# First mixture in six sub-runs of 400 and 384 tokens instead of eight of 300

## The chip, the cores and the metric

The kernel runs on one core of one Trainium2 chip. The core's engines are TensorE (PE, with PEld for its weight loads), VectorE (DVE), ScalarE (ACT), GpSimd (POOL) and SyncE (SP, which issues most transfers). The metric is the device time of one launch in microseconds (us). Three timed runs of the kernel before gave 945.01, 948.21 and 948.75 us, median 948.21.

## The reference

Attention with a memory term (4 batches, 8 heads, 576 positions, head size 64), then a mixture of 8 experts over the 2304 tokens, each token through one expert only, then a dense gated layer over all tokens:

```
local   = softmax(causal(q k^T / 8)) v
mem_out = (phi(q) M_prev) / (phi(q) z_prev + 1e-6)      # phi(x) = elu(x) + 1
x       = sigmoid(beta) * mem_out + (1 - sigmoid(beta)) * local      # -> 2304 x 512
logits  = x w_gate + modality_bias[modality_id]
e       = argmax(logits);   p = softmax(logits)[e]
out1    = p * (relu(x w1[e]) w2[e])                     # 512 -> 1024 -> 512
out     = (silu(out1 w_gate2) * (out1 w_val)) w_out     # 512 -> 1536 -> 512
```

With the inputs that are timed, all tokens fall to two of the eight experts, 1173 to the one and 1131 to the other.

## The kernel before

Three stages follow one another on the core. Matrix products are made of fp32 values split in two parts, high and low (three matmuls for one product: high by high, high by low, low by high), so a "block" of work on TensorE comes in threes.

Stage 1 is the attention: 16 pairs of heads, four for each batch. When a batch's pairs are done, `route` computes its gate logits, chooses the expert of each token and writes row numbers, sorted by expert, to a table in device memory (`idsE`). The order of all work is set when the program is built: class `Sched` is a planner which holds every piece with an engine, a planned duration, the pieces it needs, the buffers it takes from pools, and a priority. It goes through planned time and writes the pieces out; each engine executes its own in that order. A table `PRM` (line 32) holds one offset of priority for each kind of piece in stage 1.

Stage 2 is the first mixture. Each chosen expert's rows are computed in `NS=4` sub-runs of `W=300` rows. After three of the four batches are routed, the expert with most rows is chosen, and the first `NE=2` of its sub-runs take rows of those three batches; so they are prepared inside stage 1, and computed while the routing of the last batch goes on. A sub-run is in two functions. `rows` (L642) loads its row numbers (L646), transposes them on TensorE (L647), gathers the rows by three indirect transfers that POOL issues (L652), transposes these on TensorE (L654), and splits them: ACT writes the high part (L657), DVE the low one (L658). `sub` (L661) walks eight blocks of the hidden layer: 12 matmuls (L682 to L684) give `h` for 128 hidden units, ACT writes `hh` (L686), DVE `hl` (L687), then 12 matmuls (L670 to L672) add the block's part to the four outputs `y`. TensorE does h0, h1, y0, h2, y1 and so on: 192 matmuls, 300 columns each. At the end the outputs leave PSUM (L693) and go to memory (L696), and the row numbers after them (L697). The function `rest` would run on, in a loop on the chip, for rows that do not fit the eight sub-runs.

The weights of the experts come in as fp32 and are split by ACT and by POOL or DVE (`split`, L620). The dense layer's weights come in a 64-bit form; twelve of these tiles are decoded in stage 2, in two halves each (`split64`, L623 to L640).

Stage 3 is the dense layer, six tiles of 384 tokens, with outputs scattered to their rows. The change leaves it alone but for the places of a few buffers.

The planner's start rule, which decides among pieces, is unchanged; the functions that the change touches follow.

Of the kernel before, what the change touches and what calls it, by code (L numbers as in the profile page):

```python
# [176 lines left out]
class Net:  # L177
    W=300; NS=4; NE=2; TN=384
    TP=16000.; US=PRM['US']
    def __init__(s,tc,A):  # L180
        s.tc=tc; s.nc=tc.nc; s.A=A
        s.B,s.H,s.S,s.D=A['q'].shape; s.HP=s.H//2; s.NP=s.B*s.HP
        s.T=s.B*s.S; s.E=A['moe_w_gate'].shape[1]; s.dm=A['moe_w_gate'].shape[0]; s.F1=A['moe_w1'].shape[2]; s.F2=A['moe2_w_gate'].shape[1]
        s.CAP=s.W*s.NS; s.R=s.T+s.CAP
# [5 lines left out]
    def consts(s,pc,pa):  # L190
# [8 lines left out]
        s.wg=T(pc,"wg",[128,4,48]); s.mi=T(pa,"mi",[128,B,5,2],I32); s.mb2=T(pa,"mb2",[128,2,E]); s.mf=T(pa,"mf",[128,2,B*5])  # L199
        s.bias=T(pc,"bias",[128,B*5,E]); s.bias2=T(pa,"bias2",[128,B*5,E]); s.cum=T(pc,"cum",[128,B*5+1,E],BF)  # L200
# [282 lines left out]
    def route(s,b):  # L483
# [105 lines left out]
    def slots(s):  # L589
# [3 lines left out]
        s.pick(7,8,3,float(s.CAP))  # L593
# [50 lines left out]
    def rows(s,row,deps,prio,ph,ps,name='',nb=None):  # L644
        nc=s.nc; sc=s.sc; n=s.W//3; it,ii,xh,xl=sc.tok('it'),sc.tok('ii'),sc.tok('xh'),sc.tok('xl'); tp0=sc.tok(ps)
        d=sc.dma(lambda: s.after('ids',nc.sync.dma_start(out=it.tile,in_=s.idsE[bass.ds(row(),s.W),:].rearrange("(a c) o -> a (c o)",a=3))),deps=deps[0],acq=[it],prio=prio,name='id'+name,ph=ph,late=4500. if ph==1 else 3500.)  # L646
        a=sc.add('PE',10,lambda: nc.tensor.transpose(tp0.tile[0:n,0:3],it.tile,s.ident[0:3,0:3]),deps=[d],acq=[tp0],use=[it],prio=prio+.1,name='it'+name,ph=ph)  # L647
# [13 lines left out]
    def sub(s,rw,w1,w2,col,prio,ph,wr,name=''):  # L661

        nc=s.nc; sc=s.sc; W=s.W; it,xh,xl,xd=rw; ys=[sc.tok(f'y{d}') for d in range(4)]; st=24600./8; NF=s.F1//128; ylast=[]
        prev=None; yT=[]
# [11 lines left out]
        for fb in range(NF):  # L676
            wh,wl,wd=w1[fb//2]; hp=sc.tok('h'); hh,hl=sc.tok('hh'),sc.tok('hl')
            def f(wh=wh,wl=wl,hp=hp,fb=fb):
                fs=slice(128*(fb%2),128*(fb%2)+128); o=hp.tile[:,0:W]
                for k in range(4):  # L680
                    H=wh.tile.rearrange("p (k f) -> p k f",k=4)[:,k,fs]; Lo=wl.tile.rearrange("p (k f) -> p k f",k=4)[:,k,fs]
                    nc.tensor.matmul(o,H,xh.tile[:,k],start=(k==0),stop=False)  # L682
                    nc.tensor.matmul(o,H,xl.tile[:,k],start=False,stop=False)  # L683
                    nc.tensor.matmul(o,Lo,xh.tile[:,k],start=False,stop=(k==3))  # L684
# [1 line left out]
            b=sc.add('ACT',ac(W),lambda hp=hp,hh=hh: nc.scalar.activation(out=hh.tile,in_=hp.tile[:,0:W],func=AF.Relu),deps=[a],acq=[hh],use=[hp],prio=prio+fb*st,name=f'hh{name},{fb}',ph=ph)  # L686
            c=sc.add('DVE',dv(W),lambda hp=hp,hh=hh,hl=hl: nc.vector.scalar_tensor_tensor(out=hl.tile,in0=hp.tile[:,0:W],scalar=0.0,in1=hh.tile.bitcast(F32),op0=ALU.max,op1=ALU.subtract),deps=[b],acq=[hl],use=[hp,hh],prio=prio+fb*st,name=f'hl{name},{fb}',ph=ph)  # L687
# [251 lines left out]
```

## Time and profile before

| what | us |
|---|---|
| median of three timed runs | 948.21 |
| the profiled execution | 954.26 |
| its span in the trace | 952.5 |
| TensorE busy | 921.6 (97%) |
| VectorE busy | 491.4 (52%) |
| ScalarE busy | 388.7 (41%) |
| GpSimd busy | 177.3 (19%) |
| stage 1, start to 247.7 | 247.7 |
| stage 2, 247.7 to 488.0 | 240.3 |
| stage 3, 488.0 to the end | 464.5 |

The profiled execution is one of its own, 6.05 us above the median of the timed ones, so its terms are counted against its own time. TensorE's matmuls are pipelined: one lasts longer than the distance to the next start, and the sum of the engine's work is read from the distance of starts.

### The profile page before, as it was taken

The page shows a single profiled execution, that of the slowest core. Times are in us where ns is not written, and L with a number is a line of the kernel's source. Part 1 is how long each engine was busy: PE and PEld are TensorE (multiplying, and loading weights), DVE is VectorE, ACT ScalarE, POOL GpSimd, SP SyncE. Part 2 cuts the span into 40 slices and gives each one's busy share as a digit, 9 for nine tenths or more (in the row PEclk, how much of TensorE's full clock was granted, in tenths as well). Part 3 has the DMA queues.
Part 4 walks back from the last instruction along what each step waited for, and adds up shares of the span by engine and source line. Part 5 has one row for each costly group of instructions (what it writes and reads, how often), then busy time and mean ns, then how long its engine had stood idle before and what let it go on. Part 6 is the DMA issues. An engine that isn't in the chain of part 4 may idle for free. (4 is left out here: it accounts for less than half of the span.)

```text
span 952.5 us, 16582 instructions
## 1 busy us (share of the span) xinstructions
PE 921.6 (97%) x6389; PEld 841.0 (88%) x6389; DVE 491.4 (52%) x1382; ACT 388.7 (41%) x902; POOL 177.3 (19%) x199
## 2 busy tenths in 40 slices
PE   8999999999899899999989999999999999999996
PEld 6787787877799899999989999999999999999995
DVE  7988888887542728832558862232223223222221
ACT  6888888788424334411424431121122112111111
POOL 3112111125427324311212220001001001001001
PEclk9999999999999999999999999999999999999999
DMA  6632437124266425441233320001001000000000
GB/s 137 135 75 53 109 85 116 28 40 150 93 83 216 144 87 172 141 144 53 84 114 123 111 65 25 1 20 47 1 0 67 1 1 34 1 1 34 1 1 34
DMA packets 93424, 67.27 MB, mean 71 GB/s; under 512 B 67514, under 2 KB 78924, under 8 KB 93341
## 3 DMA queue, kind: packets, MB, share of 16 engines
q1 hardware_dynamic: 88797, 56.37, 23.0%
q0 software_dynamic: 4544, 9.79, 3.2%
q8 instruction: 52, 0.85, 0.4%
q14 instruction: 31, 0.25, 0.1%
HBM read 51.65 MB, written 14.49 MB: 69 GB/s over the span
## 5 line engine op out<-in xcount | busy, mean ns | idle before, releaser
L796 DVE SCALAR_TENSOR_TENSOR X<-X,gv 128x384 f32<-128x384 f32 x72 | 39.9, 554 | 186.4 <-ACT X L795 186.4
L787 PE MATMUL gv<-xx,wB 128*128 128x384 f32 x384 | 130.7, 340 | 2.0 <-PEq L822 2.0
L789 PE MATMUL gv<-xx,wB 128*128 128x384 f32 x384 | 130.7, 340 | 0.0
L788 PE MATMUL gv<-xx,wB 128*128 128x384 f32 x384 | 130.7, 340 | 0.0
L795 ACT ACTIVATE X<-gv 128x384 f32<-128x384 f32 x72 | 35.4, 491 | 190.0 <-PE gv L789 176.9
L422 ACT ACTIVATE PF<-SS,sm 128x256 f32<-128x256 f32 (+1 forms) x144 | 87.3, 609 | 9.5 <-DVE sm L410 7.0
L606 POOL DMA_INDIRECT out_dram<-X,ii x18 | 17.5, 973 | 368.8 <-ACT X L814 366.2
L787 PEld LDWEIGHTS gv<-xx,wB 128*128 128x128 f32 x384 | 72.5, 189 | 4.3 <-issue 2.2
L788 PEld LDWEIGHTS gv<-xx,wB 128*128 128x128 f32 x384 | 72.5, 189 | 2.0
L789 PEld LDWEIGHTS gv<-xx,wB 128*128 128x128 f32 x384 | 72.6, 189 | 0.0
L687 DVE SCALAR_TENSOR_TENSOR hl<-h,hh 128x300 fp32r<-128x300 f32 x64 | 30.0, 468 | 81.9 <-ACT hh L686 81.6
L797 DVE TENSOR_TENSOR X<-X,gv 128x384 f32<-128x384 f32 x72 | 39.9, 554 | 61.1 <-PE gv L789 60.9
L410 DVE CUSTOM_DVE_ANT_0 SS<-ps,mk 128x256 f32<-128x256 f32 (+2 forms) x128 | 64.8, 518 | 7.9 <-PE ps L402 5.7
L686 ACT ACTIVATE hh<-h 128x300 fp32r<-128x300 f32 x64 | 26.7, 418 | 91.3 <-PE h L684 85.5
L432 PE MATMUL tp<-ident,PF 128*128 128x128 f32 x384 | 61.7, 281 | 1.7 <-ACT pt L438 1.3
L438 ACT ACTIVATE pt<-tp 128x512 f32<-128x512 f32 (+2 forms) x112 | 55.0, 506 | 16.1 <-PE tp L432 13.9
L683 PE MATMUL h<-xx,wB 128*128 128x300 f32 x192 | 57.6, 300 | 1.5 <-DVE xx L658 1.5
L682 PE MATMUL h<-xx,wB 128*128 128x300 f32 x192 | 57.9, 302 | 0.0
L684 PE MATMUL h<-xx,wB 128*128 128x300 f32 x192 | 57.6, 300 | 0.0
L807 PE MATMUL po<-wB,al 128*128 128x512 f32 x144 | 56.7, 394 | 0.0
L432 PEld LDWEIGHTS tp<-ident,PF 128*128 128x128 f32 x384 | 43.5, 141 | 8.8 <-ACT pt L438 3.6
L670 PE MATMUL y<-hh,wB 128*128 128x300 f32 x160 | 49.1, 307 | 1.0 <-DVE X L693 1.0
(287 smaller groups left out, 2337.8 us busy)
## 6 DMA issues: line engine op xcount, KB each, us to landing
raw<-in_moe_w_dram SPq DMA_DIRECT2D x16, 512.0 KB
raw<-in_moe_w_gate_dram SPq DMA_DIRECT2D x12, 512.0 KB
raw<-in_moe_w_val_dram SPq DMA_DIRECT2D x12, 512.0 KB
raw<-in_moe_w_out_dram SPq DMA_DIRECT2D x12, 512.0 KB
yT<-X SPq DMA_DIRECT2D x8, 600.0 KB
X<-yT SPq DMA_DIRECT2D x6, 768.0 KB
kn<-in_k_dram SPq DMA_DIRECT2D x32, 128.0 KB
qn<-in_q_dram SPq DMA_DIRECT2D x32, 128.0 KB
```

Source lines behind the costliest of these rows:

```text
L410: def f(Sp=Sp,SS=SS,i=i,N=N,c=c,so=so): nc.vector.tensor_tensor_reduce(out=SS.tile[:,0:N],in0=Sp.tile[:,so:so+N],in1=s.mk[:,512-128*i:512- ...
L422: def f(SS=SS,PF=PF,N=N,c=c): nc.scalar.activation(out=PF.tile[:,0:N],in_=SS.tile[:,0:N],func=AF.Exp,scale=-1.0,bias=sm.tile[:,c:c+1],accu ...
L432: for j in range(m+1): nc.tensor.transpose(tp.tile[:,128*j:128*j+128],PF.tile[:,128*j:128*j+128],s.ident)
L438: else: cps.append(add('ACT',ac(W),lambda pc=pc,tv=tv: nc.scalar.activation(out=pc(),in_=tv(),func=AF.Copy),deps=[Tt],prio=pu+2*US,name=f' ...
L670: nc.tensor.matmul(o,H,hh.tile,start=(fb==0),stop=False)
L682: nc.tensor.matmul(o,H,xh.tile[:,k],start=(k==0),stop=False)
L683: nc.tensor.matmul(o,H,xl.tile[:,k],start=False,stop=False)
L684: nc.tensor.matmul(o,Lo,xh.tile[:,k],start=False,stop=(k==3))
L787: nc.tensor.matmul(o,H,yh.tile[:,k],start=(k==0),stop=False)
L788: nc.tensor.matmul(o,H,yl.tile[:,k],start=False,stop=False)
L789: nc.tensor.matmul(o,Lo,yh.tile[:,k],start=False,stop=(k==3))
L807: nc.tensor.matmul(o,lv()[:,c],H,start=False,stop=(f==NF-1))
```

## The change

The first mixture's sub-runs become 400 rows wide and three for each expert. The second expert's take 384 rows (`W1`), so all six hold 3 x 400 and 3 x 384 rows where eight held 300 each. The rows of a sub-run come in `G` groups of at most 128: four of 100, or three of 128. The write of the row numbers (`iw`) now waits for the load of the same numbers and the write before it, and its priority is six tenths of a sub-run ahead of the sub-run. The pools are dealt out anew for the wider tiles: two `hh` and two `hl` instead of three, two `it` instead of three, the buffers of the last stage in other places of the tiles X0 and X1. The gate's matmul has 32 columns instead of 48. All offsets in `PRM` are new, so the whole order of stage 1 is.

```diff
...
-    'AV,5':6, 'AV,7':-5.67, 'AV,8':-4.47, 'S,0':4.42, 'S,2':5.94, 'S,3':4.15, 'S,8':3.99, 'T,0':-5.64, 'T,1':-5.59, 'T,2':-3.75, 'T,3':-5.07,
+    'AV,5':-5.84, 'AV,7':-5.21, 'AV,8':-1.56, 'S,0':5.11, 'S,2':5.25, 'S,3':5.41, 'S,8':4.95, 'T,0':-6, 'T,1':-3.05, 'T,2':-1.59, 'T,3':-3.46,
...
-    W=300; NS=4; NE=2; TN=384
+    W=400; NS=3; NE=2; TN=384
...
-        s.CAP=s.W*s.NS; s.R=s.T+s.CAP
+        s.CAP=s.W*s.NS; s.R=s.T+s.CAP; s.W1=s.T//2//s.NS; s.CAP1=s.W1*s.NS
...
-        s.wg=T(pc,"wg",[128,4,48]); s.mi=T(pa,"mi",[128,B,5,2],I32); s.mb2=T(pa,"mb2",[128,2,E]); s.mf=T(pa,"mf",[128,2,B*5])
+        s.wg=T(pc,"wg",[128,4,32]); s.mi=T(pa,"mi",[128,B,5,2],I32); s.mb2=T(pa,"mb2",[128,2,E]); s.mf=T(pa,"mf",[128,2,B*5])
...
-                    for c in range(0,m,64): nc.tensor.matmul(lg.tile[c:c+64,0:48],xt.tile[:,k,c:c+64],s.wg[:,k],start=(k==0),stop=(k==3))
+                    for c in range(0,m,64): nc.tensor.matmul(lg.tile[c:c+64,0:32],xt.tile[:,k,c:c+64],s.wg[:,k],start=(k==0),stop=(k==3))
...
-        s.pick(7,8,3,float(s.CAP))
+        s.pick(7,8,3,float(s.CAP1))
...
-        nc=s.nc; sc=s.sc; n=s.W//3; it,ii,xh,xl=sc.tok('it'),sc.tok('ii'),sc.tok('xh'),sc.tok('xl'); tp0=sc.tok(ps)
+        nc=s.nc; sc=s.sc; W=W or s.W; G=-(-W//128); n=W//G; it,ii,xh,xl=sc.tok('it'),sc.tok('ii'),sc.tok('xh'),sc.tok('xl'); tp0=sc.tok(ps)
...
-        for j in range(3):
+        for j in range(G):
...
+        iw=sc.dma(lambda: nc.sync.dma_start(out=s.ids[bass.ds(col(),W),:].rearrange("(a c) o -> a (c o)",a=G),in_=it.tile[0:G,0:n]),deps=[idd]+wr[-1:],use=[it],prio=prio-.6*s.ST,name='iw'+name,ph=ph)
...
-        wr.append(sc.dma(lambda: nc.sync.dma_start(out=s.ids[bass.ds(col(),W),:].rearrange("(a c) o -> a (c o)",a=3),in_=it.tile),deps=wr[-1:]+wr[-2:-1],use=[it],prio=prio+9.3*st,name='iw'+name,ph=ph))
+        wr.append(iw)
...
-        for q in range(8):
-            if q>=2: s.rw[q]=s.rows(R[q],([rg]+sd,xw),st*(q-.7),2,'xp',f'{q}')
-            s.sub(s.rw[q],s.w1[q//4],s.w2[q//4],C[q],st*q,2,s.wr,f'{q}')
+        for q in range(2*NS):
+            if q>=NE: s.rw[q]=s.rows(R[q],([rg]+sd,xw),S2*(q-.7),2,'xp',f'{q}',W=W if q<NS else W1)
+            s.sub(s.rw[q],s.w1[q//NS],s.w2[q//NS],C[q],S2*q,2,s.wr,f'{q}')
...
-        s.tiles(pc,'it',3,[3,W//3]); s.tiles(pc,'ii',2,[128,3],I32)
-        xx=[pc.tile([128,4,TN],F32R,name=f"xx{i}") for i in range(4)]
+        s.tiles(pc,'it',2,[4,128]); s.tiles(pc,'ii',2,[128,4],I32)
+        xx=[pc.tile([128,4*W],F32R,name=f"xx{i}") for i in range(4)]
...
-            s.tiles(p2,'hh',3,[128,W],F32R); s.tiles(p2,'hl',3,[128,W],F32R)
+            s.tiles(p2,'hh',2,[128,W],F32R); s.tiles(p2,'hl',2,[128,W],F32R)
...
```
In the order on POOL at the end of stage 1 before, the rows of the second prepared sub-run (row numbers ii1) are gathered in three pieces, with splits of weights (L620) behind them; X1 is the last batch's output, xr the gathered rows:

```order
L472 TENSOR_TENSOR X1_84<-t10_133,t20_134 128x4x128
L652 DMA xr0_98<-xg_59,ii0_78 100x512
L652 DMA xr1_99<-xg_59,ii0_78 100x512
L652 DMA xr2_100<-xg_59,ii0_78 100x512
L652 DMA xr3_101<-xg_59,ii1_79 100x512
L620 TENSOR_TENSOR w3_69<-raw0_73,w0_66 128x1024
L472 TENSOR_TENSOR X1_84<-t10_133,t20_134 128x4x128
L652 DMA xr0_98<-xg_59,ii1_79 100x512
L652 DMA xr1_99<-xg_59,ii1_79 100x512
L620 TENSOR_TENSOR w5_71<-raw1_74,w1_67 128x1024
L620 TENSOR_TENSOR HL_72<-raw2_104,w2_68 128x1024
L472 TENSOR_TENSOR X1_84<-t10_133,t20_134 128x4x128
```

The same place on POOL after, with line numbers of the changed file (gathers L654, splits L621):

```order
L473 TENSOR_TENSOR X1_83<-t10_132,t20_133 128x4x128
L654 DMA xr0_97<-xg_59,ii0_77 100x512
L654 DMA xr1_98<-xg_59,ii0_77 100x512
L654 DMA xr2_99<-xg_59,ii0_77 100x512
L654 DMA xr3_100<-xg_59,ii0_77 100x512
L473 TENSOR_TENSOR X1_83<-t10_132,t20_133 128x4x128
L621 TENSOR_TENSOR w1_67<-raw0_73,w0_66 128x1024
L621 TENSOR_TENSOR w3_69<-raw1_74,w2_68 128x1024
L654 DMA xr0_97<-xg_59,ii1_78 100x512
L654 DMA xr1_98<-xg_59,ii1_78 100x512
L654 DMA xr2_99<-xg_59,ii1_78 100x512
L654 DMA xr3_100<-xg_59,ii1_78 100x512
```

All four gathers of the second sub-run now stand behind two splits, where one of three stood ahead of one split and the other two ahead of the next two.

On TensorE, the end of stage 1 before; L654 transposes gathered rows, L432 to L445 are the attention's last pieces, L682 is the first matmul of stage 2:

```order
L654 MATMUL ps2_142<-ident_148,xr3_101 128x100 x4
L441 MATMUL mm0_147<-ident_148,PF0_122 128x128
L432 MATMUL tp0_143<-ident_148,PF0_122 128x128 x4
L467 MATMUL tp1_144<-ident_148,oT0_132 128x128 x4
L445 MATMUL mm0_147<-vn10_110,pt41_131 64x64 x10
L654 MATMUL ps1_141<-ident_148,xr0_98 128x100 x4
L654 MATMUL ps0_140<-ident_148,xr1_99 128x100 x4
L491 MATMUL xp0_3377<-ident_148,X1_84 128x128 x4
L682 MATMUL h0_3375<-xx0_80,w0_66 128x300
```

And after:

```order
L656 MATMUL ps0_139<-ident_147,xr3_100 128x100 x4
L442 MATMUL mm0_146<-ident_147,PF0_121 128x128
L433 MATMUL tp0_142<-ident_147,PF0_121 128x128 x4
L468 MATMUL tp1_143<-ident_147,oT0_131 128x128 x4
L446 MATMUL mm0_146<-vn10_109,pt41_130 64x64 x10
L656 MATMUL ps1_140<-ident_147,xr0_97 128x100 x4
L656 MATMUL ps2_141<-ident_147,xr1_98 128x100 x4
L656 MATMUL ps0_139<-ident_147,xr2_99 128x100 x4
L656 MATMUL ps1_140<-ident_147,xr3_100 128x100 x4
L492 MATMUL xp0_3390<-ident_147,X1_83 128x128 x4
L685 MATMUL h0_3388<-xx0_79,w0_66 128x400
```

Between the attention's last piece and the first matmul of stage 2 stand four groups of transposes instead of two.

## Rows read from the trace of the kernel before

**Rows 1.** Stretches: us, busy of PE, PEld, DVE, ACT, POOL (instructions), clock, DMA, GB/s.
```profile
0.00:225.00 225.00, 217.69 (x2160) 174.03 (x2161) 189.61 (x807) 186.66 (x511) 46.93 (x80) 1.00 0.43 92
225.00:247.70 22.70, 17.19 (x151) 14.36 (x149) 16.33 (x41) 13.88 (x32) 14.58 (x10) 0.85 0.37 114
247.70:488.00 240.30, 230.47 (x1706) 225.65 (x1707) 122.20 (x255) 86.92 (x170) 80.69 (x63) 0.99 0.42 117
```

**Rows 2.** Timeline of PE: start, us, operation, count [idle before <-releaser].
```profile
270.35 0.30 PE L670 MATMUL y<-hh,wB 128*128 128x300 f32 x1
...
275.33 0.30 PE L682 MATMUL h<-xx,wB 128*128 128x300 f32 x1
...
519.20 0.34 PE L787 MATMUL gv<-xx,wB 128*128 128x384 f32 x1
...
523.44 0.39 PE L805 MATMUL po<-wB,ah 128*128 128x512 f32 x1
```

**Rows 3.** Timeline of PE: transposes of gathered rows and of full tiles.
```profile
182.28 1.04 PE L491 MATMUL ps<-ident,X 128*128 128x128 f32 x8
...
384.15 0.85 PE L654 MATMUL xp<-ident,xr 100*128 100x100 f32 x8
```

**Rows 4.** Timeline of PE: two waits for the third sub-run's rows.
```profile
288.39 0.21 PE L647 MATMUL xp<-ident,it 3*100 3x3 f32 x1 [1.32 <-DMA it<-idsE]
...
310.30 0.41 PE L682 MATMUL h<-xx,w 128*128 128x300 f32 x1 [0.46 <-ACT xx L657]
```

**Rows 5.** Timeline of DVE, tail of stage 1.
```profile
233.11 0.16 DVE L382 TENSOR_TENSOR dn<-dn,gate 128x6 f32<-128x6 f32 x1
...
236.34 4.77 DVE L382 TENSOR_TENSOR dn<-dn,gate 128x4 f32<-128x4 f32 x1
```

**Rows 6.** Timeline of POOL, tail of stage 1.
```profile
234.06 1.01 POOL L652 DMA_INDIRECT xr<-xg,ii  x1 [2.05 <-PE ps L654]
235.38 1.01 POOL L652 DMA_INDIRECT xr<-xg,ii  x1 [0.31 <-PE ps L654]
236.42 2.37 POOL L620 TENSOR_TENSOR w<-raw,w 128x1024 fp32r<-128x1024 f32 x1
238.73 2.35 POOL L620 TENSOR_TENSOR HL<-raw,w 128x1024 fp32r<-128x1024 f32 x1
```

**Rows 7.** Timeline of PE, tail of stage 1.
```profile
234.84 0.64 PE L377 MATMUL mm<-mb,qp 128*128 128x130 f32 x4
...
238.72 0.56 PE L654 MATMUL ps<-ident,xr 100*128 100x100 f32 x4
242.07 0.30 PE L441 MATMUL mm<-ident,PF 128*128 128x128 f32 x1 [2.79 <-DVE t L390]
...
245.16 1.18 PE L654 MATMUL ps<-ident,xr 100*128 100x100 f32 x8
```

**Rows 8.** Two stretches at a lower granted clock, columns as in rows 1.
```profile
242.36:245.77 3.41, 3.41 (x33) 2.96 (x31) 2.48 (x9) 1.54 (x2) 1.00 (x1) 0.50 0.38 121
317.46:320.87 3.41, 3.41 (x16) 3.41 (x15) 3.02 (x4) 0.58 (x2) 1.45 (x1) 0.50 0.69 216
```

**Rows 9.** Timeline of DVE, of POOL and of PE around 314.
```profile
312.24 3.14 DVE L634 TENSOR_SCALAR X<-X 128x512 int32<-128x512 int32 x1
...
312.69 2.41 POOL L620 TENSOR_TENSOR wB<-raw,wB 128x1024 fp32r<-128x1024 f32 x1
...
316.54 0.40 PE L672 MATMUL y<-hl,w 128*128 128x300 f32 x1 [1.92 <-DVE hl L687]
```

**Rows 10.** Page's groups: busy, mean ns | idle before and its releaser.
```profile
L687 DVE SCALAR_TENSOR_TENSOR hl<-h,hh 128x300 fp32r<-128x300 f32 x64 | 30.0, 468 | 81.9 <-ACT hh L686 81.6
...
L686 ACT ACTIVATE hh<-h 128x300 fp32r<-128x300 f32 x64 | 26.7, 418 | 91.3 <-PE h L684 85.5
```

**Rows 11.** Line L682 with its shapes: count, ns least/median/most, first and last start.
```profile
L682 PE MATMUL h<-xx,wB x192: 295/299/408, 265.3 to 480.4; 128*128 128x300 f32 x192
...
L682 PE MATMUL h<-xx,w x64: 295/301/453, 247.7 to 352.0; 128*128 128x300 f32 x64
```

More of the change, by code (lines that the diff above doesn't have):

```diff
@@ L32 @@
 PRM={'US': 1807, 'slack': 69, 'ps': (3, 2, 1, 1, 1), 'dcopy': (0,), 'off':{
[10 rows of a table removed]
[5 rows of a table added]
+    'gate':4.72, 'gx':5.91, 'ic':1.15, 'id':6, 'it':4.18, 'kHi':-0.09, 'kLo':3.5, 'kT':0.25, 'ldk':-0.67, 'ldm':-6, 'ldq':0.47, 'ldv':4.2, 'ldz':-1.77,
[4 rows of a table added]
 NW=24; NC=4
@@ L642, in w2src, with rows @@
     def w2src(s,er,j): w=s.A['moe_w2'].rearrange("e f d -> (e f) d"); return lambda: w[bass.ds(s.er[er]*s.F1+256*j,256),:].rearrange("(k p) d -> p k d",p=128)
-    def rows(s,row,deps,prio,ph,ps,name='',nb=None):
-        nc=s.nc; sc=s.sc; n=s.W//3; it,ii,xh,xl=sc.tok('it'),sc.tok('ii'),sc.tok('xh'),sc.tok('xl'); tp0=sc.tok(ps)
-        d=sc.dma(lambda: s.after('ids',nc.sync.dma_start(out=it.tile,in_=s.idsE[bass.ds(row(),s.W),:].rearrange("(a c) o -> a (c o)",a=3))),deps=deps[0],acq=[it],prio=prio,name='id'+name,ph=ph,late=4500. if ph==1 else 3500.)
-        a=sc.add('PE',10,lambda: nc.tensor.transpose(tp0.tile[0:n,0:3],it.tile,s.ident[0:3,0:3]),deps=[d],acq=[tp0],use=[it],prio=prio+.1,name='it'+name,ph=ph)
-        a=sc.add('DVE',75,lambda: nc.vector.tensor_copy(ii.tile[0:n],tp0.tile[0:n,0:3]),deps=[a],acq=[ii],use=[tp0],prio=prio+.2,name='ic'+name,ph=ph)
+    def rows(s,row,deps,prio,ph,ps,name='',nb=None,W=None):
+        nc=s.nc; sc=s.sc; W=W or s.W; G=-(-W//128); n=W//G; it,ii,xh,xl=sc.tok('it'),sc.tok('ii'),sc.tok('xh'),sc.tok('xl'); tp0=sc.tok(ps)
+        d=sc.dma(lambda: s.after('ids',nc.sync.dma_start(out=it.tile[0:G,0:n],in_=s.idsE[bass.ds(row(),W),:].rearrange("(a c) o -> a (c o)",a=G))),deps=deps[0],acq=[it],prio=prio,name='id'+name,ph=ph,late=4500. if ph==1 else 3500.)
+        a=sc.add('PE',10,lambda: nc.tensor.transpose(tp0.tile[0:n,0:G],it.tile[0:G,0:n],s.ident[0:G,0:G]),deps=[d],acq=[tp0],use=[it],prio=prio+.1,name='it'+name,ph=ph)
+        a=sc.add('DVE',75,lambda: nc.vector.tensor_copy(ii.tile[0:n,0:G],tp0.tile[0:n,0:G]),deps=[a],acq=[ii],use=[tp0],prio=prio+.2,name='ic'+name,ph=ph)
@@ L649, in rows @@
         dd=[]
-        for j in range(3):
+        wv=lambda t: t.tile[:,0:4*W].rearrange("p (k c) -> p k c",k=4)
+        for j in range(G):
             xr=sc.tok('xr'); tp=sc.tok(ps); cs=slice(n*j,n*j+n)
-            g=sc.dma(lambda j=j,xr=xr: nc.gpsimd.indirect_dma_start(out=xr.tile[0:n],out_offset=None,in_=s.xg if nb is None else s.xg[0:1+nb*s.S],in_offset=bass.IndirectOffsetOnAxis(ap=ii.tile[0:n,j:j+1],axis=0)),eng='POOL',deps=[a]+deps[1],acq=[xr],use=[ii],prio=prio+.3,nbytes=204800,name='gx'+name,ph=ph,late=3500.)
+            g=sc.dma(lambda j=j,xr=xr: nc.gpsimd.indirect_dma_start(out=xr.tile[0:n],out_offset=None,in_=s.xg if nb is None else s.xg[0:1+nb*s.S],in_offset=bass.IndirectOffsetOnAxis(ap=ii.tile[0:n,j:j+1],axis=0)),eng='POOL',deps=[a]+deps[1],acq=[xr],use=[ii],prio=prio+.3,nbytes=2048*n,name='gx'+name,ph=ph,late=3500.)
@@ L681, in f @@
                     H=wh.tile.rearrange("p (k f) -> p k f",k=4)[:,k,fs]; Lo=wl.tile.rearrange("p (k f) -> p k f",k=4)[:,k,fs]
[L682 to L684 removed]
+                    nc.tensor.matmul(o,H,wv(xh)[:,k],start=(k==0),stop=False)
+                    nc.tensor.matmul(o,H,wv(xl)[:,k],start=False,stop=False)
+                    nc.tensor.matmul(o,Lo,wv(xh)[:,k],start=False,stop=(k==3))
             a=sc.add('PE',12*pr(W),f,deps=xd+wd,acq=[hp],use=[xh,xl,wh,wl],prio=prio+fb*st,name=f'h{name},{fb}',ph=ph)
[L686 to L687 removed]
+            b=sc.add('ACT',ac(W),lambda hp=hp,hh=hh: nc.scalar.activation(out=hh.tile[:,0:W],in_=hp.tile[:,0:W],func=AF.Relu),deps=[a],acq=[hh],use=[hp],prio=prio+fb*st,name=f'hh{name},{fb}',ph=ph)
+            c=sc.add('DVE',dv(W),lambda hp=hp,hh=hh,hl=hl: nc.vector.scalar_tensor_tensor(out=hl.tile[:,0:W],in0=hp.tile[:,0:W],scalar=0.0,in1=hh.tile.bitcast(F32)[:,0:W],op0=ALU.max,op1=ALU.subtract),deps=[b],acq=[hl],use=[hp,hh],prio=prio+fb*st,name=f'hl{name},{fb}',ph=ph)
             if prev: ylast=yf(*prev)
@@ L753, in plan2 @@
             s.wt.append(r)
-    npre=12; nearly=4; pdec=[3.2+.4*i for i in range(8)]+[7.2+.1*i for i in range(10)]
+    ST=32800.; npre=12; nearly=4; pdec=[3.2+.4*i for i in range(8)]+[7.2+.1*i for i in range(10)]
     def ytile(s,t,deps,p0,p1,ph):
@@ L898 @@
             p3=P(c3,"p3"); pp=P(c3,"pp3",space=PSUM)
-            t3=max(sc.free.values()); U=1024; sc.pools['raw']=sc.pools['raw'][:2]
-            sc.pool('th',[u[:,U+TN*i:U+TN*i+TN] for i in range(2)]); sc.pool('ob',[u[:,U+2*TN:U+2*TN+512],v[:,4*TN:4*TN+512],v[:,4*TN+512:4*TN+1024]])
+            t3=max(sc.free.values()); U=512; sc.pools['raw']=sc.pools['raw'][:2]
+            sc.pool('th',[u[:,U+TN*i:U+TN*i+TN] for i in range(2)]); sc.pool('ob',[u[:,U+2*TN:U+2*TN+512],u[:,U+2*TN+512:U+2*TN+1024],v[:,4*TN+512:4*TN+1024]])
             sc.pool('ah',[p3.tile([128,TN],F32R,name='ah0'),hl[:,2048:2048+TN]]); s.tiles(p3,'al',2,[128,TN],F32R)
```

45 lines of the change are left out of this document (23 added, 22 removed), and 17 rows, old and new, of the table PRM.

## The prediction

> **What bounds the kernel now.** I read the table of stretches first: in stage 1 up to 225 us TensorE is busy 217.69 of 225.00 us, in the tail of that stage, 225.00 to 247.70, 17.19 of 22.70, in stage 2 230.47 of 240.30 [rows 1]. So TensorE sets the end, the first mixture is nearly all TensorE work, and what is idle lies mostly in the tail of stage 1 (5.5 us in 22.7) and in stage 2 (9.8 us in 240). The reader should see that stage 2 can only become shorter by fewer or cheaper matmul columns or by taking out one of its few waits. The timeline of TensorE was read next, for the distance from one start to the next at each width [rows 2, 3] and for the waits [rows 4, 7, 9], then the timelines of DVE and POOL to see why two waits are so long [rows 5, 6, 9], last the groups of the page and the line L682 [rows 10, 11].
>
> **Columns.** From 270.35 to 275.33 stand 36 matmuls of 300 columns: 138.3 ns each. From 519.20 to 523.44 stand 24 of 384 columns: 176.7 ns each [rows 2]. Between them a column costs (176.7 - 138.3)/84 = 0.457 ns, and almost nothing is left that is paid per matmul: 138.3 - 300 x 0.457 = 1.2 ns. So 400 columns cost 176.7 + 16 x 0.457 = 184.0 ns. Before there are 8 x 192 = 1536 matmuls x 138.3 = 212.4 us. After there are 576 x 184.0 + 576 x 176.7 = 106.0 + 101.8 = 207.8 us. Difference **-4.7 us**. Of this nearly all is the columns (2400 before, 2352 after: 48 x 192 x 0.457 = 4.2 us), only 0.5 us the smaller count of matmuls. No width of 400 is in the trace: at the 300's price by column, 138.3/300 = 0.461, the 400 cost 184.4 ns and the term is -4.4; with the slope alone it is -4.7. Both ends are close and on the path, as TensorE waits little.
>
> **Transposes of rows.** Eight of 100 by 100 took 0.85 us, eight of 128 by 128 took 1.04 us from the first's start to the last's end [rows 3], so four cost 0.43 and 0.52. Stage 2 before prepares six sub-runs in three groups: 18 x 0.43 = 7.7. After it prepares one in four groups of 100 and three in three groups of 128: 4 x 0.43 + 9 x 0.52 = 6.4. Stage 1 gets two groups more, +0.9. With two transposes of row numbers fewer, taken at 0.1 in all since the next matmuls start under their ends, the term is **-0.5 us** (bounds -0.8 and -0.2, with the 0.21 of [rows 4] for each of the two or with nothing). The copies by ACT and DVE lie beside TensorE.
>
> **Waits of the third sub-run.** The third sub-run takes its numbers from the routing of the last batch, and TensorE waits 1.32 us for their load at 288.39 and 0.46 us for the rows at 310.30 [rows 4]. After, that sub-run begins 2 x 192 x (184.0 - 138.3) ns = 17.5 us later against the same routing, so both waits are under other work: **-1.8 us**. What is late next there is the weights of the second expert and the decoded tiles, which is the fourth part. Bounds: -1.8 and 0, as the planner may put the load later by the same time.
>
> **The blocked DVE.** L382 multiplies 128x4 values and took 4.77 us, where the same line on 128x6 took 0.16 [rows 5]. It ends at 241.11; the two splits on POOL run from 236.42 to 238.79 and from 238.73 to 241.08 [rows 6]. TensorE waited 2.79 us, to 242.07, for what hangs on it [rows 7], and then ran 3.41 us at half the granted clock (1.2 of 2.4 GHz); so it did after a wait of 1.92 us at 316.54, which has the same pattern: the DVE's L634 took 3.14 us while a POOL split took 2.41 [rows 8, 9]. At half the clock 3.41 us do the work of 1.71, so each costs up to 1.7 us besides the wait.
>
> In the order after, both splits stand right behind the addition to X1 on POOL, and all four gathers of the second sub-run behind them. POOL came free at 234.06 - 2.05 = 232.01 before [rows 6]; there the splits would run from 232.0 to 232.0 + 2.37 + 2.35 = 236.7. The first gate multiplication on DVE was due at 233.11 [rows 5] and is caught: by the row it is blocked until both splits are done, to 236.7. TensorE's next matmuls of that memory term began at 234.84 [rows 7]; they come after DVE, at about 237.6, 2.8 us later. The next gate multiplication then meets no split, so the old wait of 2.79 goes: the lock is moved, not removed. POOL's gathers wait for row buffers that TensorE reads behind this, to about 238.2; four at a pitch of 235.38 - 234.06 = 1.32 end at 238.2 + 3 x 1.32 + 1.01 = 243.2. A gather that ended at 236.39 was read by 238.72, so landing takes at most 2.3: 245.5. A group of transposes is 0.56, and before the last group ended at 246.34 and the stage at 247.70, 1.36 later [rows 1, 7]: stage 2 begins at 247.4 in place of 247.7. Tail: **-0.3 us**. Bounds: if both wait and half clock fall away, -2.8 - 1.7 = -4.5; if a second pair of splits catches DVE once more (4.8) and TensorE runs its slow 3.41 us again (1.7), about +6.
>
> On who is blocked for how long, the row shows L382 held until the second split's end although it asked 0.08 us before the first. The Trainium skill (SBUF — State Buffer, "Who interferes with whom") says that a DVE instruction with two SBUF inputs and a GpSimd instruction which reads SBUF exclude each other, and that the one that issued first has the ports for its whole instruction. The trace agrees on the exclusion (4.77 us), not on who is first. By that rule the DVE would get its turn after one split, at 234.4; TensorE would not be late, the gathers would start at 236.7, and stage 2 at 246.0: the sum would be 1.4 us smaller, 939.6.
>
> **Stage 2's own locks.** 24 halves of weights are decoded in stage 2 before and after, each with DVE work that a POOL split can catch. One made TensorE wait 1.92 us [rows 9]. Which are caught after, no row tells; I take **0**, bounds -3.6 (that wait and its half clock gone) and +14 (four more). Two hl buffers instead of three cost nothing: TensorE does h0, h1, y0, h2, so y0 has read the buffer before h2 is even computed, whose hl takes it next. An h group lasts 12 x 184 ns = 2.2 us instead of 1.66, and hh and hl, 418 and 468 ns at 300 columns [rows 10], grow by a third, 0.89 to 1.18 us: the slack for hl grows from 0.77 to 1.0 us.
>
> **The rest.** The write of row numbers now stands ahead of its sub-run on SP instead of behind the write of yT; behind it on SP are loads of the second set of weights, first used at 265.3 [rows 11], some 18 us into stage 2, so I take 0. No row prices an issue on SP; six at POOL's 1.01 [rows 6] would be 6 us if that cover were gone. There is nothing to gain, since no wait of TensorE was for these writes. The gate's matmuls of 32 columns instead of 48, 2304/64 x 4 = 144 of them: by the column 144 x 16 x 0.457 ns = -1.1 us, but 100 columns of a transpose cost 0.85/8 = 106 ns [rows 3], more than twice their columns' price, so at few columns these don't set the time: I take 0, bounds -1.1 and 0. The new order of stage 1 has the same matmuls; idle is 225.00 - 217.69 = 7.3 us up to 225 [rows 1], so it can give back at most that and I take **0**, bounds -5 and +7 (as much again).
>
> **Sum.** -4.7 - 0.5 - 1.8 - 0.3 + 0 + 0 + 0 = -7.3 us on the profiled execution's 954.26, 946.96. That run is 0.6% above the median of the timed runs, 948.21, so the share is taken: 948.21 x (1 - 7.3/954.26) = **941.0 us**.
>
> **Rivals.**
> (a) A larger gain. The lock at 236.34 and the one at 312.24 both go, with their half clock: -4.5 and -3.6 in place of -0.3 and 0, so about 933. For it: both hang on where a split meets one DVE instruction. Against it: POOL's two splits are back to back again.
> (b) No change. The tail or the rewritten stage 1 gives up what the columns save: +6 of the gain, 947. For it: every offset is new, the planner's times do not know of the lock; all four gathers wait behind two splits. Against it: stage 1 had only 7.3 us of idle before, and the same pieces.
> (c) Slower. The decode in stage 2 is caught more often. With the second expert's splits and the decode moved against wider sub-runs, a lock of 3.1 us exceeds the slack of 1.0 us for hl, and TensorE waits 1.92 and loses up to 1.7 each time [rows 8, 9]. It decides from four more caught halves of the 24: 4 x 3.6 = 14.4, 941.0 + 14.3 = 955.3. Against it: one in 24 was caught so far and the slack grew.
> (d) The change does not do what it says: the loop for the rest runs once. Before, L682 runs 192 + 64 = 256 = 8 sub-runs x 8 blocks x 4 times [rows 11], so the loop was not taken. The second expert's room falls from 1200 to 1152, its tokens are 1131. If the loop ran, 192 matmuls of 184 ns and more are added, 35 us, 976.
>
> **How the numbers follow.** The measurement tells from no change what differs by more than 0.5%, 4.7 us: faster is under 943.5, slower over 952.9. The forecast with a spread of 936 to 946 has 0.55, of which 0.41 lies under 943.5; (a) 0.12, 930 to 936, all of it faster; (b) 0.20, 946 to 952, all of it no change; (c) 0.10 and (d) 0.03, both slower. So faster 0.53, no change 0.34, slower 0.13. The range 932 to 952 leaves out the lower half of (a) and all of (c) and (d), 0.19.
>
> **What would show it.** Starts of matmuls 184 ns and 177 ns apart in stage 2, 1152 of them; no waits for row numbers at the third sub-run; DVE's gate multiplication held to the end of the second split in the tail, and stage 2's begin within a few us of 247.7. The forecast is wrong if stage 2 is not shorter by about 6 us, if waits for hl come up in it several times, or if stage 1 is longer by more than 3 us.

## The result and the profile after

The changed kernel took 935.65 us (median of four, 931.27 to 937.79), the kernel before 947.43 beside it: ratio 0.9873, 95% interval 0.9827 to 0.9919. Two further timings gave 0.9851 (0.9830 to 0.9873) and 0.9856 (0.9830 to 0.9883). That is 12 to 16 us less, where 7.3 were forecast. The profiled execution took 931.27 us, its span is 929.5.

The table of stretches after, columns as in [rows 1]: stage 1 up to 222, its tail, stage 2 to the last matmul of y, stage 3; then one stretch at the lower clock.

```profile
0.00:222.00 222.00, 216.78 (x2167) 174.24 (x2167) 194.71 (x810) 187.37 (x513) 46.99 (x81) 1.00 0.48 93
222.00:244.03 22.03, 14.85 (x150) 12.11 (x149) 15.23 (x39) 13.79 (x31) 16.93 (x12) 0.96 0.47 135
244.03:466.70 222.67, 221.03 (x1301) 215.95 (x1299) 119.36 (x228) 82.54 (x147) 73.84 (x57) 1.00 0.40 122
466.70:929.50 462.80, 452.75 (x2378) 424.31 (x2377) 165.20 (x282) 101.59 (x191) 35.87 (x48) 1.00 0.11 35
242.39:245.80 3.41, 3.18 (x13) 3.20 (x14) 0.57 (x1) 1.89 (x3) 0.76 (x1) 0.50 0.42 140
```

Stage 2 has lost nearly all its idle: 222.67 - 221.03 = 1.6 us, where it was 9.8 [rows 1]. Of the 9.8, 2.0 are the wait at the branch ahead of stage 3, which ends at 487.82 and which the row of stage 2 after leaves out, as it ends with the last matmul of y; without it 7.9 stand against 1.6. The tail of stage 1 has more, 7.2 us in place of 5.5.

The timeline of TensorE in stage 2 after; columns as in [rows 2]:

```profile
270.52 0.34 PE L685 MATMUL h<-xx,wB 128*128 128x400 f32 x1
...
288.02 0.34 PE L685 MATMUL h<-xx,w 128*128 128x400 f32 x1
...
442.71 0.34 PE L685 MATMUL h<-xx,wB 128*128 128x384 f32 x1
...
451.14 0.34 PE L685 MATMUL h<-xx,wB 128*128 128x384 f32 x1
```

Between the first two stand 96 matmuls, 182.3 ns each, between the last two 48, 175.6 ns each. The column still costs 0.456 ns.

All waits of TensorE in stage 2 after (us in total, times, longest); two are left, besides the branch ahead of stage 3 (the line with gv), and both stand at the first sub-run of the second expert, at 358.03 and 359.31:

```profile
PE gv L790 <- PEq L825: 2.0, 1, 2.0
PE h L686 <- DVE xx L660: 0.8, 1, 0.8
PE h L685 <- ACT xx L659: 0.7, 1, 0.7
```

The same list of the kernel before, from its second profile (run before2):

```profile
PE y L672 <- DVE hl L687: 2.9, 3, 1.9
PE gv L787 <- PEq L822: 2.4, 1, 2.4
PE xp L647 <- DMA it<-idsE: 2.4, 1, 2.4
PE h L683 <- DVE xx L658: 1.7, 2, 1.5
PE y L670 <- DVE X L693: 1.0, 1, 1.0
PE h L682 <- DVE xx L658: 0.9, 1, 0.9
PE h L682 <- ACT xx L657: 0.5, 1, 0.5
PE y L670 <- ACT hh L686: 0.3, 1, 0.3
```

Of the 1.7 us for xx from DVE, 0.2 stand at the third sub-run and 1.5 at the first sub-run of the second expert. The 0.9 stand ahead of the first matmul of stage 2, so they belong to the tail of stage 1.

The tail of stage 1 after, on POOL, on DVE and on TensorE, to compare with [rows 5 to 7]:

```profile
224.70 4.69 POOL L621 TENSOR_TENSOR w<-raw,w 128x1024 fp32r<-128x1024 f32 x2
...
235.72 1.00 POOL L654 DMA_INDIRECT xr<-xg,ii  x1 [0.63 <-PE mm L442]
```

```profile
226.00 3.42 DVE L383 TENSOR_TENSOR dn<-dn,gate 128x6 f32<-128x6 f32 x1
...
231.45 0.16 DVE L383 TENSOR_TENSOR dn<-dn,gate 128x4 f32<-128x4 f32 x1
```

```profile
230.14 0.71 PE L378 MATMUL mm<-mb,qp 128*128 128x130 f32 x4 [3.15 <-DVE t L385]
...
242.62 0.90 PE L656 MATMUL ps<-ident,xr 100*128 100x100 f32 x4 [3.24 <-DMA xr<-xg,ii]
```

The lock moved as forecast: the first gate multiplication is held to 229.42, when the second split ends (229.39); the next one takes 0.16. What was not forecast is the wait for the last gather, issued by 236.72 and read only at 242.62.

The sums below are worked out from the starts of TensorE's instructions in each trace; before2 and after2 are second profiles of the two kernels, narrow is an experiment below. For stage 2, every matmul of the sub-runs at the median distance of its shape ("columns"), the distances of transposes and the gate ("other"), what distances over 0.4 us have above the median ("gaps": waits, with the branch), what shorter ones have above it at half clock and elsewhere.

| us | stage 1 | columns | other | gaps | half clock | rest | stage 3 |
|---|---|---|---|---|---|---|---|
| before | 247.7 | 212.0 | 11.9 | 11.1 | 1.5 | 3.6 | 464.7 |
| before2 | 245.6 | 212.0 | 11.9 | 13.0 | 2.8 | 3.7 | 464.7 |
| after | 244.0 | 206.2 | 10.0 | 4.7 | 0.6 | 3.2 | 460.7 |
| after2 | 247.1 | 206.2 | 10.0 | 3.7 | 0.0 | 3.5 | 461.1 |
| narrow | 248.0 | 207.4 | 11.6 | 13.2 | 2.8 | 5.0 | 458.3 |

Between the means of the first two and of the next two rows: columns -5.8, other -1.9, gaps -7.9, half clock -1.9, stage 3 -3.8, stage 1 -1.1. The sum, some 23 us, is more than the medians show: both profiles of before are of about 955 us, and those of the changed kernel are the fastest of their sets (931.27 and 933.37). The kernel before had medians of 947.43, 956.25, 950.12 and 949.41 in the four sets of runs, the changed one 935.65, 934.55 and 935.59 in three of them. Why the kernel before takes 947 us in one set and 956 in another is open. The table tells which terms fell, and not how many of their microseconds a given median has. The half clock is the least settled of them: a third profile of the changed kernel (run after3, 940.32 us) has two such stretches in stage 2, from 251.4 to 254.8 and from 367.5 to 370.9.

### The profile page after: what moved, and what is told of

Same layout as the page of the kernel before. It is cut to its first block, busy times and chain, and to the rows that moved or that the text cites. A ratio compares the mean times of both kernels' runs of the same rounds, so it can differ in the third digit from the quotient of the medians.

```text
span 929.5 us, 15721 instructions
## 1 busy us (share of the span) xinstructions
PE 905.4 (97%) x5991; PEld 826.6 (89%) x5991; DVE 494.5 (53%) x1357; ACT 385.3 (41%) x879; POOL 173.6 (19%) x197
## 4 chain that ended last, share of the span: by engine, by line
issue 31%; PE 17%; POOL 2%; POOLq 0%; ACT 0%
PE gv L790 4%; PE gv L791 4%; PE gv L792 4%; PE po L808 2%; PE po L809 2%; PE po L810 2%; POOL out_dram L607 1%; POOL gap L606 0%; POOLq L937 0%; ACT X L817 0%; POOLq L607 0%; PE gv L774 0%
## 5 line engine op out<-in xcount | busy, mean ns | idle before, releaser
L690 DVE SCALAR_TENSOR_TENSOR hl<-h,hh 128x400 fp32r<-128x400 f32 (+1 forms) x48 | 27.0, 562 | 58.8 <-ACT hh L689 58.7
L689 ACT ACTIVATE hh<-h 128x400 fp32r<-128x400 f32 (+1 forms) x48 | 23.7, 494 | 78.2 <-PE h L687 78.0
L685 PE MATMUL h<-xx,wB 128*128 128x384 f32 (+1 forms) x144 | 49.6, 345 | 0.7 <-ACT xx L659 0.7
L639 POOL TENSOR_TENSOR wB<-X,wB 128x512 fp32r<-128x512 f32 x24 | 32.5, 1356 | 93.8 <-ACT wB L638 61.8
L686 PE MATMUL h<-xx,wB 128*128 128x384 f32 (+1 forms) x144 | 49.1, 341 | 0.8 <-DVE xx L660 0.8
L687 PE MATMUL h<-xx,wB 128*128 128x384 f32 (+1 forms) x144 | 49.0, 340 | 0.0
```

What stands on the lines that cost most here:

```text
L685: nc.tensor.matmul(o,H,wv(xh)[:,k],start=(k==0),stop=False)
L686: nc.tensor.matmul(o,H,wv(xl)[:,k],start=False,stop=False)
L687: nc.tensor.matmul(o,Lo,wv(xh)[:,k],start=False,stop=(k==3))
```

## The experiments

**The kernel before, once more.** 

> The kernel before again, for a second profiled execution (the first was 6.05 us above the median of the timed runs, the changed kernel's 4.4 us below its own). Theory A (part of the 23 us between the two profiles is chance of one execution: which waits are followed by a stretch at half clock, which DVE work is caught by a split on POOL): this profile is shorter than 954.26, near 948, the order and the sum of columns the same, with other or shorter waits. Rival B (the first profile is what the kernel always does): 952 to 956 again, with the waits of 2.79 and 1.92 us in the same places. Ratio to before 1.00 in both.

 Measured 955.51 us, ratio 1.0002 (0.9985 to 1.0019), the same waits at the same places. Theory A falls in this form: the first profile is no odd execution. Four stretches at half clock again, one of them at another place (287.6, where the first profile had one at 228.7):

```profile
239.80:243.20 3.40, 3.08 (x27) 2.79 (x29) 2.58 (x8) 1.54 (x2) 0.12 (x1) 0.51 0.23 51
287.60:291.00 3.40, 3.40 (x14) 3.38 (x15) 0.46 (x2) 1.36 (x2) 3.26 (x2) 0.50 0.61 169
318.30:321.70 3.40, 3.40 (x16) 3.40 (x16) 2.82 (x4) 0.57 (x2) 1.44 (x1) 0.51 0.71 214
489.00:492.40 3.40, 3.40 (x11) 3.40 (x12) 0.00 (x0) 0.00 (x0) 0.00 (x0) 0.50 0.51 176
```

Each stands at the end of a wait of TensorE or just behind it: the gate, the row numbers of the third sub-run, hl, the branch.

**The old offsets with the new sub-runs.**
```diff
-PRM={... 'AV,5':-5.84, 'AV,7':-5.21, ...}
+PRM={... 'AV,5':6, 'AV,7':-5.67, ...}
```


> The changed kernel with the offsets PRM of the kernel before: six wide sub-runs, memory and early row numbers as changed, stage 1 planned with the old numbers. Theory A (columns -4.7 to -5.3, transposes -0.5, waits of the third sub-run -1.8 come from the sub-runs; the rest of the 11.8 us, about 4, is from the new order): 947.4 - 7.5 = 940, ratio 0.992. Rival B (the new order of stage 1 gives nearly all): 946, ratio 0.999. Rival C (the order gives nothing, all is the sub-runs): 936, ratio 0.988.

 Measured 933.98 us, ratio 0.9766 (0.9742 to 0.9791). The sub-runs alone give the whole gain, more than theory A gave them; rival B falls, and what came is rival C. (The kernel before had its highest median in this set, 956.25.) On the same chip as the changed kernel: 

> The changed kernel with the old offsets, on the same chip as the changed kernel. Theory A (the new offsets of stage 1 give nothing with the new sub-runs; the gain is all from the six sub-runs): within 3 us of the changed kernel, as 934.0 and 934.6 us on two chips suggest. Rival (the new offsets cost, as they did in the kernel before, 0.8%): 5 us or more below the changed kernel. Rival (they give a part of the gain): 3 us or more above it.

 933.21 us, ratio 0.9830 (0.9803 to 0.9857), beside 935.59 of the changed kernel (

> The changed kernel once more, the reference for the three beside it on the same chip: 934 to 936 us.

): 2.4 us below, within the 3 us of theory A. The new order gives nothing here.

**The new offsets with the old sub-runs.** The other way round, PRM of the changed kernel in the kernel before. 

> The kernel before with only the new offsets PRM: eight sub-runs of 300. Theory A: about 4 us less than before, 943, ratio 0.996. Rival B (the order gives nearly all): 937, ratio 0.989. Rival C (the order gives nothing, or is good only with the new sub-runs): 947 or more, ratio 1.00.

 Measured 962.90 us, ratio 1.0077 (1.0052 to 1.0101): 7 us slower. Rival C was right. Its stage 1 is 252.6 us, with longer waits than in the old order (there 0.3 for HL, 0.8 for qp at L345, 0.9 to 1.7 at L362):

```profile
PE prep L351 <- DVE HL L343: 3.6, 2, 3.3
PE prep L345 <- DVE qp L369: 2.2, 2, 1.4
PE prep L362 <- DVE qp L359: 2.1, 2, 1.6
```

This profile also ran 27.3 us at half clock ahead of its last microseconds, where each of the two of before ran 13.6. How much of the 7 us is waits and how much half clock is not separated.

**Eight sub-runs with the changed kernel's columns.**
```diff
-    W=400; NS=3; NE=2; TN=384
+    W=300; NS=4; NE=2; TN=384
...
-    ST=32800.; npre=12; nearly=4; ...
+    ST=24600.; npre=12; nearly=4; ...
```
(W1 becomes 288; the tiles xx keep the size that stage 3 needs.) 

> The changed kernel with eight sub-runs again, four of 300 and four of 288, so the same 2352 columns in 1536 matmuls instead of 1152. Theory A (TensorE pays by the column, 0.457 ns, and next to nothing by the matmul): stage 2's matmuls cost 0.5 us more, transposes about the same, the third sub-run's waits come back in part (0 to 1.8): 936 to 938, ratio 0.989 to 0.990. Rival D (what helps is fewer and longer matmuls, fewer changes from block to block, the longer cover of ACT and DVE): most of stage 2's gain is lost, 942 or more, ratio over 0.995.

 Measured 952.31 us, ratio 0.9962 (0.9941 to 0.9983). This is the result that decides most. The columns are the same and cost 207.4 us against 206.2, as theory A said, and yet the gain is gone: rival D has the size. The new offsets cost time with eight sub-runs, as the run before this one shows, so stage 2 is the place to look: it is 240.0 us long, as before (240.1 and 243.3), and not 224.7 or 223.4. Most of the waits are back (the y that waits to be copied out is not):

```profile
PE y L675 <- DVE hl L690: 3.3, 3, 1.9
PE xp L648 <- DMA it<-idsE: 3.2, 1, 3.2
PE gv L790 <- DVEq L825: 3.1, 1, 3.1
PE h L686 <- DVE xx L660: 1.7, 2, 1.5
PE h L685 <- ACT xx L659: 0.5, 1, 0.5
```

and behind two of them, and behind the branch, the stretches at half clock:

```profile
290.61:294.02 3.41, 3.41 (x14) 3.39 (x15) 0.61 (x2) 1.37 (x2) 3.29 (x2) 0.50 0.54 172
321.33:324.74 3.41, 3.41 (x16) 3.41 (x15) 2.83 (x4) 0.57 (x2) 1.46 (x1) 0.50 0.75 233
488.60:492.00 3.40, 3.40 (x13) 3.40 (x11) 0.00 (x0) 0.07 (x1) 0.67 (x1) 0.50 0.51 176
```

The same holds over all the runs of this text. Stage 2, from its first matmul to the first of stage 3, takes 223.4 to 227.7 us in the eight profiles with six sub-runs and 239.7 to 245.6 in the six with eight, whichever offsets they have. None of the eight has a wait over 0.15 us for hl or for row numbers in stage 2; each of the six has both (hl 0.9 to 3.5 us, row numbers 1.3 to 4.1). The half clock in stage 2 does not part them so well: 0 to 8.9 us in the first, 3.4 to 10.2 in the second. That the width does it and not the smaller number of sub-runs, which comes with it, is argued from what waits; no run changes one without the other.

In this kernel DVE's decode is caught by a split as in [rows 9], with 3.12 us; the changed kernel's is caught too, with 1.66 us, and TensorE does not wait. The longest hold of the decode in the changed kernel's stage 2 is 2.2 us (374.7), also without a wait. Whether the wider block would outlast one of 3.1 us, no run shows. First narrow, DVE and POOL, then after2, DVE and POOL:

```profile
315.92 3.12 DVE L635 TENSOR_SCALAR X<-X 128x512 int32<-128x512 int32 x1
```
```profile
316.34 2.41 POOL L621 TENSOR_TENSOR wB<-raw,wB 128x1024 fp32r<-128x1024 f32 x1
```
```profile
311.76 0.57 DVE L690 SCALAR_TENSOR_TENSOR hl<-h,hh 128x400 fp32r<-128x400 f32 x1 [1.50 <-ACT hh L689]
312.31 1.66 DVE L634 TENSOR_SCALAR X<-X 128x512 f32<-128x512 f32 x1
```
```profile
311.26 2.42 POOL L621 TENSOR_TENSOR wB<-raw,wB 128x1024 fp32r<-128x1024 f32 x1
```

**One split of the kernel before on DVE.** A first try moved the wrong split:
```diff
-            s.w2[1].append(s.split(s.w2src(1,j),st*(1.5+.6*j),2,'POOL',[rg],f'2,1,{j}'))
+            s.w2[1].append(s.split(s.w2src(1,j),st*(1.5+.6*j),2,'POOL' if j<3 else 'DVE',[rg],f'2,1,{j}'))
```


> The kernel before with one of the second expert's eight splits, the last, on DVE instead of POOL: the one that ran at 312.69 beside the DVE work of 3.14 us. Theory A (that split blocks DVE, hl is late, TensorE waits 1.92 us and then runs a stretch at half clock): the longest wait for hl falls under 1 us, the half-clock stretch near 317 goes, stage 2 is 2 to 3.6 us shorter, ratio 0.996 to 0.998. Rival (the wait is not the split's): wait and stretch stay, ratio 1.000.

 Measured 952.42 us, ratio 1.0025 (1.0014 to 1.0035). The split at 311.27 was still on POOL, the L634 beside it took 3.15, the wait of 1.9 stayed; it tells nothing on the theory. The same edit on w1, `'POOL' if j<3 else 'DVE'` in the line above, moves the right one. 

> The kernel before with the split that ran on POOL at 312.69 on DVE (the earlier experiment had moved the one after it). Theory A (that split blocks DVE's decode, hl is late): the L634 of 3.14 us is back at 0.43, the longest wait for hl is under 1 us, stage 2 is 2 to 3.6 us shorter; ratio 0.996 to 0.998. Rival (DVE is only late by its own work, which grows by 1.23 us): the wait stays or another of its size comes.

 Measured 948.36 us, ratio 0.9985 (0.9968 to 1.0001). DVE at this place, and TensorE's wait for hl:

```profile
310.14 0.42 DVE L634 TENSOR_SCALAR X<-X 128x512 int32<-128x512 int32 x1
```
```profile
PE y L672 <- DVE hl L687: 0.9, 2, 0.7
```

The split on POOL is shown to be the cause of the wait. The gain of 1.4 us is under the 2 to 3.6 expected and not clear of noise: the other waits are all there, and this profile has as many microseconds at half clock (13.7) as before, in other places.

**The tail: splits on DVE.**
```diff
-...'POOL' if ph==1 or i%2 else 'DVE',[rg],f'{nm},0,{j}'))
+...'DVE' if ph==1 or i%2==0 else 'POOL',[rg],f'{nm},0,{j}'))
```


> The changed kernel with the four weight splits of stage 1 on DVE instead of POOL. Theory A (POOL splits block DVE's gate multiplication, TensorE waits 3.15 us for it at 230.14): that wait goes, L383 on 128x6 takes about 0.2 us instead of 3.42; the end of stage 1 moves by at most 3 us less, since the last gather's landing is late too: ratio to before 0.001 to 0.004 below the changed kernel's. Rival (the last gather bounds the tail, whatever DVE does): no change of the tail, the wait for the gather grows by what the other loses, time within 1 us of the changed kernel.

 Measured 930.49 us, ratio 0.9793 (0.9777 to 0.9808), beside 934.55 and 0.9851 of the changed kernel on the same chip (

> The changed kernel again, a second profile, against the kernel before on the same chip as the runs beside it. Theory A: ratio between 0.977 (what the old order with the new sub-runs gave) and 0.987 (first timing): the gain is the columns, about 5 us, plus waits in stage 2 that no longer occur, each with its stretch at half clock; one to three such stretches before the end, where the kernel before has four. Rival C (the new order alone costs, as in the kernel before with the new offsets, where it lost 0.8%): ratio 0.98 or more, stage 1 longer than with the old order (245.3 us).

). So 0.6% less, a little more than theory A gave. The gate multiplication is free, and no wait for a gather is left in this tail either (waits of 0.7 to 1.7 us for DVE and ACT are):

```profile
230.11 0.15 DVE L383 TENSOR_TENSOR dn<-dn,gate 128x6 f32<-128x6 f32 x1
...
234.19 0.15 DVE L383 TENSOR_TENSOR dn<-dn,gate 128x4 f32<-128x4 f32 x1
```

**The tail: weight loads held.**
```diff
-...,[rg],f'{nm},0,{j}'))
+...,[rg]+(s.rw[1][3] if ph==2 else []),f'{nm},0,{j}'))
```


> The changed kernel with the weight loads planned in stage 2 held until the second sub-run's rows are split. Theory A (the last gather of the tail, issued by 236.72 and landed only at 242.6, shared the transfer engines with two weight loads of 512 KB; before, a gather landed within 2.3 us): the wait of 3.24 us for xr goes to under 0.7, stage 1 ends 2 to 3 us earlier; ratio 0.002 to 0.003 below the changed kernel's, unless the weights are late for h4. Rival (the gather is late by its own descriptors, POOL splits beside it): the wait stays at 3 us.

 Measured 938.88 us, ratio 0.9896 (0.9866 to 0.9927), with a wait of 3.47 us for xr. The rival is not shown by that: the planner's dependence changed the order on SP and put no wait on the chip. The first of the loads went out at 238.68, ahead of the last gather (239.78), and the transfer engines were as full as before, in the last column but one (the share of the DMA engines that is busy):

```profile
242.00:243.00 1.00, 0.70 (x9) 0.51 (x6) 0.56 (x2) 0.95 (x3) 1.00 (x2) 1.00 1.02 343
243.00:244.00 1.00, 0.00 (x0) 0.00 (x0) 1.00 (x3) 0.34 (x1) 1.00 (x1) 1.00 1.09 318
...
245.00:246.00 1.00, 0.00 (x0) 0.00 (x0) 0.00 (x0) 0.00 (x0) 1.00 (x1) 1.00 0.09 29
```

The gather was read at 246.17, after this load had passed. With the splits on DVE the share falls to 0.02 by 238, three microseconds after the last gather's issue (234.74), and nothing waits. Both agree with a gather that shares the engines with weight loads; that the loads alone do it is argued, not shown.

**Both together.** The old offsets with the splits on DVE. 

> The changed kernel with the old offsets and with the four weight splits of stage 1 on DVE. Theory A (the wait behind the gate multiplication and the stretch at half clock after it go in this order too, and without the splits POOL's gathers start sooner): 3 to 6 us below the changed kernel, as the splits on DVE gave with the new offsets (0.58%). Rival (with the old offsets TensorE waits only 1.7 us for the gather and 1.5 for the addition to X in the tail, so there is less to win): within 2 us of the kernel with the old offsets.

 Measured 931.48 us, ratio 0.9817 (0.9791 to 0.9842), 1.7 us below the old offsets alone: the rival was right, there was less to win. The best versions are this one and the changed kernel with its splits on DVE, some 4 us below the changed kernel; which of the two is better, two chips do not tell.

## Why the prediction was right, point by point

**Columns (-4.7).** Right, and a little short: 182.3 and 175.6 ns instead of 184.0 and 176.7, -5.8 to -6.2 us.

**Transposes (-0.5).** "Other" fell by 1.9; the sign was right.

**Waits of the third sub-run (-1.8).** Both went, and narrow, which starts that sub-run 65.9 us into stage 2 instead of 75.6 to 76.4, has both back, the longer one with 3.2 us.

**The blocked DVE in the tail (-0.3).** Every step of the mechanism came: held to the second split's end, TensorE 3.15 us late (2.8 forecast), the old wait gone. One size was wrong: a gather's landing "at most 2.3" us was read where the DMA share was 0.29 to 0.47 (236 to 239 before), and took 5.9 us from the issue's end (236.72 to 242.62) at a DMA share of 0.88 to 1.07 between 238 and 241:

```profile
238.00:239.00 1.00, 0.45 (x6) 0.29 (x5) 0.56 (x2) 0.90 (x2) 1.00 (x2) 1.00 1.07 303
239.00:240.00 1.00, 0.38 (x4) 0.19 (x3) 0.63 (x3) 0.50 (x1) 1.00 (x1) 1.00 0.98 341
240.00:241.00 1.00, 0.00 (x0) 0.00 (x0) 0.53 (x1) 0.00 (x0) 1.00 (x2) 1.00 0.88 302
```

On the rule of the Trainium skill (SBUF — State Buffer, "Who interferes with whom"): the trace again agrees with the exclusion and not with a turn after one split: L383 began at 226.00, inside the first of two splits from 224.70 to 229.39, and ended at 229.42. But in narrow, and likewise in neworder, the same instruction beside the same pair of splits did get its turn after the first, which ends at half of their 4.72 us, about 236.2; TensorE waited 0.2 us there:

```profile
233.86 4.72 POOL L621 TENSOR_TENSOR w<-raw,w 128x1024 fp32r<-128x1024 f32 x2
```
```profile
235.60 0.67 DVE L383 TENSOR_TENSOR dn<-dn,gate 128x6 f32<-128x6 f32 x1
```

So the step "blocked until both splits are done" came out, but it was read from one row and is not what always happens; what decides is open (last section).

**Stage 2's own locks (0).** This is the term that was mis-sized. It had the bound of -3.6 and the sentence that the slack for hl grows from 0.77 to 1.0 us, and the sum took nothing for it. Measured, the gaps of stage 2 fell by 7.9 us, of which the third sub-run is 1.8 to 2.9; the rest is mainly hl (2.8 and 2.9 to 0) and the y that waits to be copied out (1.0 to 0). The wait for the rows at the second expert's first sub-run, 1.5 us before, did not go: it is 0.7 and 0.8 after. Of all these the prediction had looked at one wait for hl only. A wider block gives hl and the row numbers more cover: with the same columns and offsets and eight sub-runs, narrow has hl (3.3) and the row numbers (3.2) back. The y's wait does not come back in it, so that one is not shown to be the width's. The half clock of stage 2 fell by 1.9 in the mean of these four profiles, but with the old offsets (run oldorder) it is 3.3 by the same count and the time no longer, so the 1.9 are not shown to go with the waits.

**The rest (0).** The new order gives nothing with the new sub-runs (-2.4 us with the old one, oldorder2) and costs 7 us with the old ones. The sum left out stage 3, which is 3.6 to 4.0 us shorter. Of this about 1.5 is the half-clock stretch that before had behind the branch (ten matmuls start 320 ns apart instead of 175); the rest goes with the distances of its matmuls (last section). The gate's matmuls start 51 ns apart (median) with 48 and with 32 columns alike, so its 0 was right. The early write of the row numbers was not tried by itself.

**Rivals.** (a), the larger gain, had the right side of the sum by another road: the tail's lock did not go. Its band, 930 to 936, holds all three medians of the changed kernel (934.55 to 935.65), while the forecast's own spread began at 936; that the time lies in the stated range is owed to the half of (a) that the range took in. (b) did not come: the gain of stage 2 was not given up in stage 1. (c) did not come; its "one in 24 was caught" counts only the one for which TensorE waited long, since in stage 2 before 14 instructions of the decode take 1.06 to 3.14 us instead of 0.42 or 0.69. (d) did not come: TensorE has 576 matmuls of each width, no loop.

## What to carry to other kernels

When an engine is full and its inputs pass through others, a wider block may pay less by what it saves than by the cover that it gives: list every wait of the stage, and ask for each whether a third more cover outlasts it, before the locks are put down as 0. A wait can cost a stretch at half clock besides (3.41 us at 1.2 GHz behind 2.36 us at 287.49 in before2), though the same wait of 1.32 us in the first profile had none behind it; a transfer's landing is priced by the share of the transfer engines at that moment, not by one that ran alone.

## What had not been expected of the hardware

DVE was often not let in between two splits that stand back to back on POOL: 3.42 us (after), 4.66 (after2) and 4.77 (before) for a multiplication of 0.16. This is so in eight of the ten profiles in which the gate multiplication meets such a pair; in narrow and neworder it got in after the first split, with 0.67 and 0.68 us. In the eight it came between 0.08 us ahead of the first split and 1.30 us into it, in the two 1.7 us into it. What decides is not shown.

And matmuls of one shape have distances that differ between the kernels: in stage 3, whose work is the same, 384 columns are 176.0 ns apart before and 175.2 after, 512 columns 232 and 231 (means past the first 5 us): 1728 x 0.8 + 647 x 1 ns = 2 us. In narrow they are 173.4 and 229.1, which makes its stage 3 shorter by 6.4 us than before's. The kernels' third stages differ in the places of buffers, so these are the likely reason; which tile makes the difference was not tried.
